# Chunk 0's keys fetched behind its other inputs, and its state sums of all batches made late in one tile

## The chip, the cores and the metric

The kernel runs on one core of one Trainium2 chip. The metric is device time in microseconds (us) of the slowest core, here the only one. A run lists its time, the span of the core in its trace (about 1.7 us less than the time) and the mean clock that TensorE was granted (1.000 is full). Runs count as fast within 1.5% of the fastest of the same kernel.

## The reference, cut to what matters

A retention layer (a linear recurrence with one decay per head), then an MLP with a leaky ReLU:

```python
# q, k, v: (4 batches, 8 heads, 768 tokens, 64)
for t in range(S):
    state = gamma * state + k[:, :, t] (outer) v[:, :, t]     # one 64x64 state per batch and head
    y[:, :, t] = scale * q[:, :, t] @ state
x = y as (3072 tokens, 512)
h = x @ w_in                       # 512 -> 2048
out = np.maximum(0.01 * h, h) @ w_out
```

## The kernel before: the parts that matter

The tokens are cut into six chunks of 128. Within a chunk the recurrence becomes matrix products: *scores* (k with q, both with dimensions first), a causal *mask* on VectorE, *values* (masked scores with decayed v), and for the chunks after it the *state sums* (k with v, both with tokens first). TensorE writes all of them into PSUM, its result memory; VectorE *takes* the values of a batch from there, times the decay, as the MLP's input x. The MLP uses a seven-product scheme, but the first products are *direct* so that they can begin with half of the inputs. Weights arrive as 64-bit floats in pieces of 512 KB and are rounded on ScalarE (three "powers" steps) and VectorE (three "mantissa" steps).

```python
def load(c, b, place=None, between=lambda: None):
    ...
    nc.sync.dma_start(out=x, in_=qk[c, b])       # 512 KB: q and k, dimensions first
    between()
    nc.sync.dma_start(out=y, in_=kv[c, b])       # 512 KB: k and v, tokens first

def state(c, b):
    y = heads.pop((c, b))[1]
    sp = for_state(sums_at[c, b])                # the free half of the bank that holds the values
    for a in range(HP) if c < NC - 1 else ():
        for j in range(2):
            nc.tensor.matmul(sp[ts(j, 64), a, :], lhsT=y[:, 0, 2 * a + j, :],
                             rhs=y[:, 1, 2 * a + j, :], start=False, stop=True, ...)

def keep_busy(n):                                # "warming": bf16 matmuls on zeros, nobody reads the result
    for _ in range(n):
        nc.tensor.matmul(idle..., lhsT=nothing[:, 0:128], rhs=nothing, ...)

# the start, in program order
load(0, 0) ; load(0, 1) ; load_piece(0) ; load_piece(1) ; load(0, 2) ; ...   # decay rates in between
keep_busy(8); score(0, 0); masked(0, 0); decay_v(0, 0, nc.vector); keep_busy(6)
values(0, 0); score(0, 1); decay_v(0, 1, nc.vector); masked(0, 1); next_powers()
state(0, 0); taken(0, 0, x); keep_busy(2)
values(0, 1); state(0, 1); taken(0, 1, x); next_powers(); next_mantissas(); next_powers()
...
keep_busy(2); decay_v(0, 2); score(0, 2); keep_busy(1); masked(0, 2)   # this decay on GpSimd
steps = direct(0, 0, x, ...); next(steps)                              # the first direct product
values(0, 2); state(0, 2); next_mantissas(); decay_v(0, 3); next(steps); ...
```

Of the kernel before, what the change touches and what calls it, by code (L numbers as in the profile page):

```python
# [23 lines left out]
def kernel(  # L24
# [35 lines left out]
    nc = tc.nc  # L60
# [13 lines left out]
    mask = const.tile([128, 128], FP32, name="mask")  # L74
    dec = const.tile([128, HP * C + H + HP], FP32, name="dec")

    st = [const.tile([128, HP, D], FP32, name=f"st{b}") for b in range(B)]



# [6 lines left out]
    def unit_tile(k, name):  # L87
        if k in LATE:
            return work.tile([128, 7, 2, 256], FP32, tag=f"late{k}", name=name)
        return const.tile([128, 7, 2, 256], FP32, name=name)  # L90
# [23 lines left out]
    heads = {}  # L114
    AHEAD = 2

    def load(c, b, place=None, between=lambda: None):

        if place is None:
            x = work.tile([128, 2, HP, C], FP32, tag="qk", bufs=AHEAD, name=f"qk_{c}_{b}")  # L120
            y = work.tile([128, 2, H, D], FP32, tag="kv", bufs=AHEAD, name=f"kv_{c}_{b}")
        else:
            flat = place.rearrange("p i k n -> p (i k n)")
            half = 2 * HP * C
            x = flat[:, 0:half].rearrange("p (s a t) -> p s a t", s=2, a=HP)
            y = flat[:, half : 2 * half].rearrange("p (s h d) -> p s h d", s=2, h=H)
        heads[c, b] = x, y
        nc.sync.dma_start(out=x, in_=qk[c, b])
        between()
        nc.sync.dma_start(out=y, in_=kv[c, b])  # L130

    def decay_v(c, b, engine=nc.gpsimd):
        v = heads[c, b][1][:, 1]
        if engine is not nc.scalar:
            engine.tensor_tensor(out=v, in0=v, in1=gk.unsqueeze(2).to_broadcast([128, H, D]),
                                 op=ALU.mult)
        else:
            for h in range(H):
                engine.activation(v[:, h], v[:, h], AF.Identity, scale=gk[:, h : h + 1])
# [6 lines left out]
    def score(c, b):  # L146

        x = heads[c, b][0]
        ps = scores[c, b] = two_banks(f"ap_{c}_{b}")
        for a in range(HP):  # L150
            for j in range(2):
                nc.tensor.matmul(ps[:, j, a, :], lhsT=x[ts(j, 64), 1, a, :],  # L152
                                 rhs=x[ts(j, 64), 0, a, :])

    def masked(c, b):
        am = work.tile([128, 2, HP, C], FP32, tag="am", bufs=2, name=f"am_{c}_{b}")
        nc.vector.tensor_tensor(  # L157
            out=am.rearrange("p j a t -> p (j a) t"),
            in0=scores[c, b].rearrange("p j a t -> p (j a) t"),
            in1=mask.unsqueeze(1).to_broadcast([128, H, C]), op=ALU.mult)  # L160
        scores[c, b] = am
# [5 lines left out]
    def reads(c, b):  # L167
        x = heads[c, b][0]
        ps = sums_at[c, b] = two_banks(f"yp_{c}_{b}")
        for j, m, i, a in pairs if c > 0 else ():  # L170
            nc.tensor.matmul(ps[ts(i, 64), j, m, :], lhsT=st[b][ts(j, 64), a, :],  # L171
                             rhs=x[ts(j, 64), 0, a, :], start=(m == 0), stop=False,
                             skip_group_check=True)

    def values(c, b):
        y, am, ps = heads[c, b][1], scores.pop((c, b)), sums_at[c, b]
        for j, m, i, a in pairs:
            nc.tensor.matmul(ps[ts(i, 64), j, m, :], lhsT=y[:, 1, 2 * a + j, :],  # L178
                             rhs=am[:, j, a, :], start=(c == 0 and m == 0), stop=True,
                             skip_group_check=True)  # L180

    def for_state(ps):
        return ps[:, 0, HP // 2 :, :].rearrange("p a (two d) -> p (a two) d", two=2)

    def state(c, b):
        y = heads.pop((c, b))[1]
        sp = for_state(sums_at[c, b])
        for a in range(HP) if c < NC - 1 else ():
            for j in range(2):
                nc.tensor.matmul(sp[ts(j, 64), a, :], lhsT=y[:, 0, 2 * a + j, :],  # L190
                                 rhs=y[:, 1, 2 * a + j, :], start=False, stop=True,
                                 skip_group_check=True)

    def taken(c, b, xb):

        ps = sums_at.pop((c, b))
        th, o = divmod(b * C, N)
        blocks = xb.rearrange("p (kh th) k n -> p kh th k n", th=2)[:, :, th, :, ds(o, C)]
        nc.vector.tensor_tensor(out=blocks, in0=ps[:, :, 0 : HP // 2, :], in1=gq, op=ALU.mult)  # L199
        sp = for_state(ps)  # L200
        if c < NC - 1:
            if c > 0:
                nc.vector.tensor_tensor(out=st[b], in0=st[b], in1=sp, op=ALU.add)
            nc.vector.tensor_tensor(out=st[b], in0=st[b] if c > 0 else sp,
                                    in1=gc.unsqueeze(2).to_broadcast([128, HP, D]), op=ALU.mult)

    def products(c, bs):
# [29 lines left out]
    def load_piece(n, place=None):  # L237
        if n >= N_PIECES:
            return
        if not f64:  # L240
            nc.sync.dma_start(out=piece(n), in_=weights[n].rearrange("p (h n) -> p h n", h=2))
            return
        if place is None:
            tag, bufs = ("raw", 3) if n < N_PIECES - 4 else (("qk", "kv")[n % 2], AHEAD)
            raws[n] = work.tile([128, W], I64, tag=tag, bufs=bufs, name=f"raw{n}")
        else:
            raws[n] = place.bitcast(I64)
        nc.sync.dma_start(out=raws[n], in_=weights[n])

    def next_powers():  # L250
        n = done["powers"]
        done["powers"] += 1
        if n < N_PIECES and f64:
            powers(n)
# [106 lines left out]
    def direct(c, u, x, g, th):  # L361


        banks = [psum.tile([128, 2, N], FP32, tag="ff", bufs=4, name=f"d{r}_{c}_{th}")
                 for r in range(2)]
        for step in range(4):
            kh, k = divmod(step, 2)
            for r in range(2):
                for i in range(2):
                    nc.tensor.matmul(  # L370
                        banks[r][:, i, :], lhsT=block(2 * u, r + 2 * kh)[:, k, ts(i, 128)],
                        rhs=x[:, 2 * kh + th, k, :], start=(step == 0 and i == 0),
                        stop=(step == 3), skip_group_check=True)
                if step == 3:
                    nc.scalar.activation(g[:, 2 * r + th], banks[r], AF.Prelu, alpha=0.01)
            yield
# [93 lines left out]
    def new_o(c):  # L470
        return work.tile([128, 4, 2, N], FP32, tag="o", bufs=2, name=f"o_{c}")
# [36 lines left out]
        return {i: [round_piece] for i in steps}  # L508

    rates = HP * C  # L510
    load(0, 0, between=lambda: nc.sync.dma_start(out=dec[:, rates:], in_=decay[:, rates:]))
    load(0, 1, between=lambda: nc.sync.dma_start(out=dec[:, :rates], in_=decay[:, :rates]))
    load_piece(0)
    load_piece(1)
    load(0, 2, new_o("in2"))
    load_piece(2)
    load_piece(3, tile_x("words").rearrange("p i k n -> p (i k n)")[:, 0 : 2 * W])
    load(0, 3, new_o("in3"))
    load(1, 0, unit_tile(LATE[2], "in10"))
    load(1, 1, unit_tile(LATE[1], "in11"))  # L520
    load(1, 2, unit_tile(LATE[0], "in12"))
    nc.vector.memset(mask, 1.0)
    nc.gpsimd.affine_select(out=mask, in_=mask, compare_op=ALU.is_ge, fill=0.0,
                            base=0, pattern=[[1, 128]], channel_multiplier=-1)
# [14 lines left out]
    def keep_busy(n):  # L539
        for _ in range(n):  # L540
            nc.tensor.matmul(idle.rearrange("p i n -> p (i n)"), lhsT=nothing[:, 0:128],
                             rhs=nothing, start=True, stop=True, skip_group_check=True)
# [2 lines left out]
    score(0, 0)  # L545
    masked(0, 0)
    decay_v(0, 0, nc.vector)
    keep_busy(6)
    reads(0, 0)
    values(0, 0)  # L550
    score(0, 1)
    decay_v(0, 1, nc.vector)
    masked(0, 1)
    next_powers()
    state(0, 0)
    taken(0, 0, x)
    keep_busy(2)
    reads(0, 1)
    values(0, 1)
    state(0, 1)  # L560
    taken(0, 1, x)
    next_powers()
    next_mantissas()
    next_powers()
    load(1, 3)
    keep_busy(2)
    decay_v(0, 2)
    score(0, 2)
    keep_busy(1)
    masked(0, 2)  # L570
    steps = direct(0, 0, x, parts[0][1], 0)
    next(steps)
    reads(0, 2)
    values(0, 2)
    state(0, 2)
    next_mantissas()
    decay_v(0, 3)
    next(steps)
    taken(0, 2, x)
    next_mantissas()  # L580
    score(0, 3)
    masked(0, 3)
    next_powers()
    next(steps)
    next_mantissas()
    reads(0, 3)
    values(0, 3)
    state(0, 3)
    decay_v(1, 0, nc.scalar)
    run(steps, {})  # L590
    taken(0, 3, x)
# [3 lines left out]
    def scored_later(b):  # L595
        score(1, b)
        masked(1, b)

    steps = direct(0, 0, x, parts[0][1], 1)
    next(steps)  # L600
    scored_later(0)
    decay_v(1, 1, nc.scalar)
    next(steps)
# [160 lines left out]
```

## Time and profile before

| | |
|---|---|
| timed runs | 673.15, 673.17, 673.52 us |
| the profiled run | 675.22 us, span 673.5, mean clock 0.997 |
| TensorE busy | 664.6 us, 99% of the span |
| first direct product starts | 18.11 us |

The prediction shows the views that carry it. One more is needed here: the timeline just ahead of the first direct product d, in the profiled run of the kernel before. A line gives start, length, engine, line of the kernel, operation, output and inputs with their shapes, and in brackets the idle time before it and what ended that.

```profile
16.09 0.39 PE L541 MATMUL idle<-t 128*128 128x512 bf16 x1
...
16.21 1.30 POOL L135 TENSOR_TENSOR o_in<-o_in,dec 128x512 f32<-128x512 f32 x1 [14.78 <-DMA o_in<-in_kv_dram]
16.71 1.34 DVE L303 SCALAR_TENSOR_TENSOR w<-w,z 128x512 f32<-128x512 f32 x1
```

TensorE's last warming matmul ends at 16.48 and d starts at 18.11, so TensorE is empty for 1.6 us. In that time GpSimd's decay of batch 2's values and VectorE's last mantissa step lie beside each other and both are long.

### The profile page before, as it was taken

The page shows a single profiled execution, that of the slowest core. Times are in us where ns is not written, and L with a number is a line of the kernel's source. Part 1 is how long each engine was busy: PE and PEld are TensorE (multiplying, and loading weights), DVE is VectorE, ACT ScalarE, POOL GpSimd, SP SyncE. Part 2 cuts the span into 40 slices and gives each one's busy share as a digit, 9 for nine tenths or more (in the row PEclk, how much of TensorE's full clock was granted, in tenths as well). Part 3 has the DMA queues.
Part 4 walks back from the last instruction along what each step waited for, and adds up shares of the span by engine and source line. Part 5 has one row for each costly group of instructions (what it writes and reads, how often), then busy time and mean ns, then how long its engine had stood idle before and what let it go on. Part 6 is the DMA issues. An engine that isn't in the chain of part 4 may idle for free.

```text
span 673.5 us, 9628 instructions
## 1 busy us (share of the span) xinstructions
PE 664.6 (99%) x4131; PEld 576.9 (86%) x4131; DVE 370.9 (55%) x566; ACT 170.4 (25%) x303; POOL 21.3 (3%) x23
## 2 busy tenths in 40 slices
PE   7999999999999999999999999999999999999997
PEld 4788888888888888888888888888888888888886
DVE  4878768889889775513733623553531444341342
ACT  2454456436352002211301211210221120221210
POOL 0100000000000110000100100100100000000000
PEclk9899999999999999999999999999999999999999
DMA  8922231231411544002102200301300000000001
GB/s 333 393 72 64 64 124 63 90 99 62 157 64 62 189 171 143 1 1 75 52 16 72 102 1 1 126 0 63 126 1 0 2 0 29 35 1 1 0 1 62
DMA packets 15306, 49.12 MB, mean 73 GB/s; under 512 B 1824, under 2 KB 1824, under 8 KB 15264
## 3 DMA queue, kind: packets, MB, share of 16 engines
q1 hardware_dynamic: 15264, 48.51, 20.2%
q8 instruction: 32, 0.52, 0.3%
q14 instruction: 10, 0.08, 0.0%
HBM read 42.21 MB, written 6.29 MB: 72 GB/s over the span
## 4 chain that ended last, share of the span: by engine, by line
PE 97%; DMA 1%; DVE 1%; SPq 0%; issue 0%; DVEq 0%
PE B_o L351 12%; PE A_o L351 12%; PE C_o L351 12%; PE C_h L351 11%; PE B_h L351 11%; PE A_h L351 11%; PE D_o L351 6%; PE D_h L351 6%; PE d L370 5%; PE yp L178 3%; PE ap L152 3%; PE yp L171 2%; PE yp L190 1%; DMA kv<-in_kv_dram 1%; DVE w L303 0%
## 5 line engine op out<-in xcount | busy, mean ns | idle before, releaser
L351 PE MATMUL A_h<-x,w 128*128 128x256 f32 x352 | 83.2, 379 | 0.0
L351 PEld LDWEIGHTS A_h<-x,w 128*128 128x128 f32 x352 | 66.9, 190 | 9.1
L351 PE MATMUL A_o<-g,w 128*128 128x256 f32 x288 | 68.0, 379 | 0.0
L383 ACT ACTIVATE g<-g 128x512 f32<-128x512 f32 x66 | 40.2, 631 | 87.7 <-DVE g L307 87.7
L351 PEld LDWEIGHTS A_o<-g,w 128*128 128x128 f32 x288 | 54.7, 190 | 7.4
L388 ACT COPY m<-A_h 128x512 f32<-128x512 f32 x22 | 12.8, 583 | 139.9 <-PE A_h L351 100.5
L307 DVE TENSOR_TENSOR m<-m,B_o 128x512 f32<-128x512 f32 x16 | 11.0, 685 | 65.9 <-PE B_o L351 65.9
L307 DVE TENSOR_TENSOR m<-m,B_h 128x512 f32<-128x512 f32 x22 | 15.1, 686 | 57.0 <-PE B_h L351 57.0
L199 DVE TENSOR_TENSOR x<-yp,dec 128x512 f32<-128x512 f32 x24 | 16.5, 689 | 50.5 <-PE yp L190 38.2
L351 PE MATMUL C_h<-t,w 128*128 128x256 f32 x176 | 42.2, 383 | 0.0
L351 PE MATMUL B_h<-x,w 128*128 128x256 f32 x176 | 42.2, 383 | 0.0
L351 PE MATMUL D_h<-t,w 128*128 128x256 f32 x176 | 41.6, 379 | 0.0
L351 PE MATMUL C_h<-x,w 128*128 128x256 f32 x176 | 41.6, 379 | 0.0
L351 PE MATMUL B_h<-t,w 128*128 128x256 f32 x176 | 41.6, 379 | 0.0
L351 PEld LDWEIGHTS D_h<-t,w 128*128 128x128 f32 x176 | 33.4, 190 | 4.5
L351 PEld LDWEIGHTS C_h<-x,w 128*128 128x128 f32 x176 | 33.4, 190 | 4.5
L351 PEld LDWEIGHTS B_h<-t,w 128*128 128x128 f32 x176 | 33.4, 190 | 4.5
L351 PEld LDWEIGHTS C_h<-t,w 128*128 128x128 f32 x176 | 32.9, 190 | 5.0
L310 DVE TENSOR_TENSOR gd<-g,gd 128x512 f32<-128x512 f32 x48 | 36.2, 753 | 1.8
L351 PEld LDWEIGHTS B_h<-x,w 128*128 128x128 f32 x176 | 32.9, 190 | 4.9 <-issue 0.3
L157 DVE TENSOR_TENSOR am<-ap,mask 128x1024 f32<-128x1024 f32 x24 | 28.6, 1220 | 12.0 <-PE ap L152 11.8
L351 PE MATMUL B_o<-gd,w 128*128 128x256 f32 x144 | 34.0, 379 | 0.0
(108 smaller groups left out, 1046.6 us busy)
## 6 DMA issues: line engine op xcount, KB each, us to landing
raw<-in_weights_dram SPq DMA_DIRECT2D x31, 512.0 KB, 3.8
qk<-in_qk_dram SPq DMA_DIRECT2D x19, 512.0 KB, 4.2
kv<-in_kv_dram SPq DMA_DIRECT2D x19, 512.0 KB, 5.2
out_dram<-o SPq DMA_DIRECT2D x24, 256.0 KB, 2.1
in<-in_qk_dram SPq DMA_DIRECT2D x3, 512.0 KB, 10.6
in<-in_kv_dram SPq DMA_DIRECT2D x3, 512.0 KB, 10.6
o_in<-in_qk_dram SPq DMA_DIRECT2D x2, 512.0 KB, 9.9
o_in<-in_kv_dram SPq DMA_DIRECT2D x2, 512.0 KB, 10.2
```

Source lines behind the costliest of these rows:

```text
L152: nc.tensor.matmul(ps[:, j, a, :], lhsT=x[ts(j, 64), 1, a, :], rhs=x[ts(j, 64), 0, a, :])
L157: nc.vector.tensor_tensor(out=am.rearrange("p j a t -> p (j a) t"), in0=scores[c, b].rearrange("p j a t -> p (j a) t"), in1=mask.unsqueeze ...
L171: nc.tensor.matmul(ps[ts(i, 64), j, m, :], lhsT=st[b][ts(j, 64), a, :], rhs=x[ts(j, 64), 0, a, :], start=(m == 0), stop=False, skip_group_ ...
L178: nc.tensor.matmul(ps[ts(i, 64), j, m, :], lhsT=y[:, 1, 2 * a + j, :], rhs=am[:, j, a, :], start=(c == 0 and m == 0), stop=True, skip_grou ...
L190: nc.tensor.matmul(sp[ts(j, 64), a, :], lhsT=y[:, 0, 2 * a + j, :], rhs=y[:, 1, 2 * a + j, :], start=False, stop=True, skip_group_check=True)
L199: nc.vector.tensor_tensor(out=blocks, in0=ps[:, :, 0 : HP // 2, :], in1=gq, op=ALU.mult)
L307: nc.vector.tensor_tensor(out=out, in0=a, in1=b, op=ALU.add)
L310: nc.vector.tensor_tensor(out=out, in0=a, in1=b, op=ALU.subtract)
L351: nc.tensor.matmul(ps[:, i, :], lhsT=block(w, sa)[:, k, ts(i, 128)], rhs=rhs[:, k, :], start=(first and i == 0 and n == 0 and k == 0), sto ...
L370: nc.tensor.matmul(banks[r][:, i, :], lhsT=block(2 * u, r + 2 * kh)[:, k, ts(i, 128)], rhs=x[:, 2 * kh + th, k, :], start=(step == 0 and i ...
L383: nc.scalar.activation(g[:, i], g[:, i], AF.Prelu, alpha=0.01)
L388: nc.scalar.copy(out=got["m1"], in_=ps)
```

## The change

Its intent: only v, not k, is needed with tokens first to get chunk 0's values out. So k (256 KB per batch) is fetched behind everything else that chunk 0 needs, and the state sums are made when all four k are there. Chunk 0 has no older state, so the four sums can be multiplied by the decay in one VectorE operation, if the four states lie in one tile. Warming matmuls, the order of the small operations and the place of two loads of chunk 1 were changed along with it. In the cut below, lines of one kind are joined with semicolons.

```diff
-    st = [const.tile([128, HP, D], FP32, name=f"st{b}") for b in range(B)]
+    states = const.tile([128, B, HP, D], FP32, name="states")
+    st = [states[:, b] for b in range(B)]
...
+    def load_v(c, b):
+        nc.sync.dma_start(out=heads[c, b][1][:, 1], in_=kv[c, b][:, 1])
+    def load_k(c, b):
+        nc.sync.dma_start(out=heads[c, b][1][:, 0], in_=kv[c, b][:, 0])
...
+    def first_states_taken(ps):
+        flat = ...
+        nc.vector.tensor_tensor(out=states, in0=flat..., in1=gc (broadcast), op=ALU.mult)
...
-    load(0, 0, ...)  load(0, 1, ...)  load_piece(0)  load_piece(1)  load(0, 2, ...)
-    load_piece(2)  load_piece(3, ...)  load(0, 3, ...)  load(1, 0, ...) ...
+    load_qk(0, 0)  (small decay row)  load_v(0, 0)  load_qk(0, 1)  (decay rates)  load_v(0, 1)
+    load_piece(0)  load_qk(0, 2)  load_v(0, 2)  load_piece(1)  load_piece(2)  load_piece(3, ...)
+    load_qk(0, 3)  load_v(0, 3)  load_k(0, 0..3)  load(1, 0, ...) ...
...
-    keep_busy(6); reads(0, 0); values(0, 0); score(0, 1); decay_v(0, 1); masked(0, 1)
-    next_powers(); state(0, 0); taken(0, 0, x); keep_busy(2); values(0, 1); state(0, 1) ...
+    keep_busy(4); score(0, 1); values(0, 0); masked(0, 1); decay_v(0, 1); keep_busy(3)
+    next_powers(); taken(0, 0, x); values(0, 1); taken(0, 1, x) ...
...
-    keep_busy(2) ... keep_busy(1)
+    score(0, 2); masked(0, 2); keep_busy(4)          # right ahead of the first direct product
...
-    decay_v(0, 3)
+    decay_v(0, 3, nc.scalar)
...
+    values(0, 3); first_state(0, sums0); first_state(1, sums0)      # behind three direct steps
...
+    first_state(2, sums0); first_state(3, sums0); first_states_taken(sums0)
```

More of the change, by code (lines that the diff above doesn't have):

```diff
@@ L115, with place_for @@
     AHEAD = 2
-    def load(c, b, place=None, between=lambda: None):
+    def place_for(c, b, place=None):
         if place is None:
@@ L127, in load, with load_qk @@
         heads[c, b] = x, y
-        nc.sync.dma_start(out=x, in_=qk[c, b])
-        between()
-        nc.sync.dma_start(out=y, in_=kv[c, b])
+    def load_qk(c, b):
+        nc.sync.dma_start(out=heads[c, b][0], in_=qk[c, b])
+    def load_v(c, b):
+        nc.sync.dma_start(out=heads[c, b][1][:, 1], in_=kv[c, b][:, 1])
+    def load_k(c, b):
+        nc.sync.dma_start(out=heads[c, b][1][:, 0], in_=kv[c, b][:, 0])
+    def load(c, b, place=None):
+        place_for(c, b, place)
+        load_qk(c, b)
+        nc.sync.dma_start(out=heads[c, b][1], in_=kv[c, b])
     def decay_v(c, b, engine=nc.gpsimd):
@@ L169, in reads @@
         ps = sums_at[c, b] = two_banks(f"yp_{c}_{b}")
-        for j, m, i, a in pairs if c > 0 else ():
+        for j, m, i, a in pairs:
             nc.tensor.matmul(ps[ts(i, 64), j, m, :], lhsT=st[b][ts(j, 64), a, :],
@@ L175, in values @@
     def values(c, b):
+        if c == 0:
+            sums_at[c, b] = two_banks(f"yp_{c}_{b}")
         y, am, ps = heads[c, b][1], scores.pop((c, b)), sums_at[c, b]
@@ L188, in state, with sums_of, first_state @@
         for a in range(HP) if c < NC - 1 else ():
-            for j in range(2):
-                nc.tensor.matmul(sp[ts(j, 64), a, :], lhsT=y[:, 0, 2 * a + j, :],
-                                 rhs=y[:, 1, 2 * a + j, :], start=False, stop=True,
-                                 skip_group_check=True)
+            sums_of(sp, y, a)
+    def sums_of(sp, y, a, start=False):
+        for j in range(2):
+            nc.tensor.matmul(sp[ts(j, 64), a, :], lhsT=y[:, 0, 2 * a + j, :],
+                             rhs=y[:, 1, 2 * a + j, :], start=start, stop=True,
+                             skip_group_check=True)
+    def first_state(b, ps):
+        y = heads.pop((0, b))[1]
+        sp = ps[:, b // 2].rearrange("p a t -> p (a t)")[:, ds(b % 2 * HP * D, HP * D)]
+        for a in range(HP):
+            sums_of(sp.rearrange("p (a d) -> p a d", d=D), y, a, start=(b % 2 == 0 and a == 0))
+    def first_states_taken(ps):
+        flat = ps.rearrange("p j a t -> p (j a t)").rearrange("p (ba d) -> p ba d", d=D)
+        nc.vector.tensor_tensor(
+            out=states,
+            in0=flat.rearrange("p (b a) d -> p b a d", b=B),
+            in1=gc.unsqueeze(1).unsqueeze(3).to_broadcast([128, B, HP, D]), op=ALU.mult)
     def taken(c, b, xb):
@@ L199, in taken @@
         nc.vector.tensor_tensor(out=blocks, in0=ps[:, :, 0 : HP // 2, :], in1=gq, op=ALU.mult)
-        sp = for_state(ps)
-        if c < NC - 1:
-            if c > 0:
-                nc.vector.tensor_tensor(out=st[b], in0=st[b], in1=sp, op=ALU.add)
-            nc.vector.tensor_tensor(out=st[b], in0=st[b] if c > 0 else sp,
+        if 0 < c < NC - 1:
+            nc.vector.tensor_tensor(out=st[b], in0=st[b], in1=for_state(ps), op=ALU.add)
+            nc.vector.tensor_tensor(out=st[b], in0=st[b],
                                     in1=gc.unsqueeze(2).to_broadcast([128, HP, D]), op=ALU.mult)
@@ L510 @@
     rates = HP * C
-    load(0, 0, between=lambda: nc.sync.dma_start(out=dec[:, rates:], in_=decay[:, rates:]))
-    load(0, 1, between=lambda: nc.sync.dma_start(out=dec[:, :rates], in_=decay[:, :rates]))
+    place_for(0, 0)
+    place_for(0, 1)
+    place_for(0, 2, new_o("in2"))
+    place_for(0, 3, new_o("in3"))
+    load_qk(0, 0)
+    nc.sync.dma_start(out=dec[:, rates:], in_=decay[:, rates:])
+    load_v(0, 0)
+    load_qk(0, 1)
+    nc.sync.dma_start(out=dec[:, :rates], in_=decay[:, :rates])
+    load_v(0, 1)
     load_piece(0)
+    load_qk(0, 2)
+    load_v(0, 2)
     load_piece(1)
-    load(0, 2, new_o("in2"))
     load_piece(2)
     load_piece(3, tile_x("words").rearrange("p i k n -> p (i k n)")[:, 0 : 2 * W])
-    load(0, 3, new_o("in3"))
+    load_qk(0, 3)
+    load_v(0, 3)
+    for b in range(B):
+        load_k(0, b)
     load(1, 0, unit_tile(LATE[2], "in10"))
     load(1, 1, unit_tile(LATE[1], "in11"))
-    load(1, 2, unit_tile(LATE[0], "in12"))
     nc.vector.memset(mask, 1.0)
@@ L547 @@
     decay_v(0, 0, nc.vector)
-    keep_busy(6)
-    reads(0, 0)
+    keep_busy(4)
+    score(0, 1)
     values(0, 0)
-    score(0, 1)
+    masked(0, 1)
     decay_v(0, 1, nc.vector)
-    masked(0, 1)
+    keep_busy(3)
     next_powers()
-    state(0, 0)
     taken(0, 0, x)
-    keep_busy(2)
-    reads(0, 1)
     values(0, 1)
-    state(0, 1)
     taken(0, 1, x)
@@ L564 @@
     next_powers()
-    load(1, 3)
-    keep_busy(2)
     decay_v(0, 2)
     score(0, 2)
-    keep_busy(1)
     masked(0, 2)
+    keep_busy(4)
     steps = direct(0, 0, x, parts[0][1], 0)
     next(steps)
-    reads(0, 2)
     values(0, 2)
-    state(0, 2)
     next_mantissas()
-    decay_v(0, 3)
+    load(1, 2, unit_tile(LATE[0], "in12"))
+    next_powers()
+    decay_v(0, 3, nc.scalar)
     next(steps)
     taken(0, 2, x)
+    score(0, 3)
     next_mantissas()
-    score(0, 3)
     masked(0, 3)
-    next_powers()
     next(steps)
     next_mantissas()
-    reads(0, 3)
+    load(1, 3)
     values(0, 3)
-    state(0, 3)
+    sums0 = two_banks("sums0")
+    first_state(0, sums0)
+    first_state(1, sums0)
     decay_v(1, 0, nc.scalar)
@@ L600 @@
     next(steps)
+    first_state(2, sums0)
+    first_state(3, sums0)
+    first_states_taken(sums0)
     scored_later(0)
```

## The prediction

> **What bounds the kernel now.** I read the page first, then the chain of waits in order of time, then busy time and granted clock in two-microsecond stretches, then the early transfers in order of time.
>
> The page: busy shares and the clock row (40 slices of 16.8 us, tenths of full clock).
>
> ```profile
> PE 664.6 (99%) x4131; PEld 576.9 (86%) x4131; DVE 370.9 (55%) x566; ACT 170.4 (25%) x303; POOL 21.3 (3%) x23
> ...
> PEclk9899999999999999999999999999999999999999
> DMA  8922231231411544002102200301300000000001
> ```
>
> TensorE is busy 99% of 673.5 us; only the first two slices have an unfilled clock or full DMA. So whatever can be won lies in the first 34 us. The chain that ended last says where (start, length, what):
>
> ```profile
> 3.12 7.89 DMA kv<-in_kv_dram
> ...
> 11.64 1.23 DVE am L157
> ...
> 12.92 1.09 PE yp L178 x16
> 14.01 0.49 PE yp L190 x16
> ...
> 15.13 0.41 DVE st L204
> 15.55 0.34 DVE w L299
> ...
> 15.92 0.71 DVE w L301
> ...
> 16.71 1.36 DVE w L303
> ...
> 18.11 3.51 PE d L370 x8
> 21.62 1.14 PE yp L178 x16
> 22.77 0.46 PE yp L190 x16
> 23.23 1.92 PE d L370 x8
> ```
>
> Until 18.11 the chain hops between a transfer, VectorE and TensorE; from 18.11 on, where the first direct product (d) starts, every later piece I looked at is TensorE. The end is therefore "time at which d starts" plus "TensorE work that is left". Two things stand out. The start waits for token-major k and v of batch 1 (the kv transfer landing at 11.0). And the first d group takes 3.51 for eight matmuls where the next takes 1.92. Busy time of PE, PEld, DVE, ACT, POOL, then clock, DMA share, GB/s:
>
> ```profile
> 14.00:16.00 2.00, 2.00 (x36) 1.45 (x30) 1.44 (x4) 1.94 (x4) 0.00 (x0) 1.00 1.03 414
> 16.00:18.00 2.00, 0.47 (x5) 0.10 (x1) 1.90 (x3) 0.77 (x2) 1.30 (x1) 1.00 1.01 397
> 18.00:20.00 2.00, 1.89 (x5) 1.59 (x6) 1.97 (x4) 1.93 (x4) 0.00 (x0) 0.61 1.04 416
> 20.00:22.00 2.00, 2.00 (x10) 1.17 (x11) 0.94 (x2) 1.26 (x2) 0.34 (x1) 0.54 1.01 401
> 22.00:24.00 2.00, 2.00 (x35) 1.85 (x31) 0.72 (x2) 0.00 (x0) 0.70 (x1) 1.00 1.05 418
> ```
>
> TensorE is nearly idle from 16 to 18, and then its clock is half for about 3.4 us. The first d product runs in that hole. DMA is saturated at some 410 GB/s, so bytes in the queue ahead of an input are time.
>
> **What the Trainium skill says.**
> 1. "TensorE: Matmul & The Clock Gate", Part 1: activity windows of about 3.4 us, free-running, each deciding between half and full clock. The trace agrees in size: the stretches above give a half-clock interval of 3.4 us, with both edges inside one two-microsecond stretch each. That its phase is free is not seen here: the three timed runs lie within 0.4 us. The page speaks of an idle window; here a window with about half its time busy was enough.
> 2. "DMA: Bandwidth & Descriptors", Specifications: transfers of at least 512 B per descriptor run at line rate. The split transfers have 2 KB rows; the 256 KB load of the decay rates has the same row size, and the stretch from 8 to 10 us, in which by the working below its last rows landed, moved 412 GB/s, the usual rate.
> 3. "SBUF — State Buffer", Who interferes with whom: VectorE with two SBUF inputs and a GpSimd operation that reads SBUF exclude each other, the later one waits. The trace agrees: the last mantissa step (L303) took 1.34 us beside a 1.30 us GpSimd decay, 0.69 alone.
> 4. "PSUM — Partial Sum Buffer", The four PSUM rules: only the first matmul in a bank clears it; sums for two batches share one bank, and the new code sets the flag only on the first. This is correctness, not time.
>
> **The change part by part.**
>
> *Loads.* Steady issues stand 1.28 us apart (9.75, 11.03, 12.31, 13.59 for 512 KB each), so 256 KB is 0.64 us. Before, the queue is qk0, small decay row, kv0, qk1, rates, kv1, weight piece 0, piece 1, qk2, kv2, pieces 2 and 3, qk3, kv3. After, each kv of chunk 0 is only its v half, qk2 and v2 stand ahead of piece 1, and the four k halves come behind v3. From kv1's landing at 11.02 backwards, qk1 landed near 9.1 (11.02 - 1.28 - 0.64). New landings: qk1 9.1 - 0.64 = 8.46; v1 8.46 + 0.64 + 0.64 = 9.74; piece 0 11.02; qk2 12.3; v2 12.9; piece 1 14.2; piece 2 15.5; piece 3 16.8; qk3 18.1; v3 18.7; the four k by 21.3. Total bytes are unchanged, so chunk 1's inputs land as before (first kv about 24.2).
>
> *The road to d.* Program order is now scores 0, four warming matmuls, scores 1, values 0, three warming, values 1, with masked 1 ahead of decay 1 on VectorE and no state sums.
> - Scores 0 start at 4.88 as before (behind the eight cold warming matmuls), mask 0 ends at 7.39; decay 0 follows without its 0.47 wait, to 8.1.
> - Scores 1: qk1 at 8.46 + 1.16 = 9.6. Mask 1 starts 0.13 after, 9.75 + 1.23 = 11.0; decay 1 starts 0.09 before that end and takes 0.69: 11.6. Values 1: 11.65 + 1.05 = 12.7.
> - The taking of batch 1: 12.75. Before, from this operation (14.53) to d (18.11) were 3.58 us. Of these 0.33 was the state product (L204), which leaves. 0.65 was the L303 collision (1.34 - 0.69). Without either, d starts at 12.75 + 2.6 = 15.35.
> - Collision again: GpSimd's decay of v2 starts at 12.9 and needs 1.04, to about 13.95. The first mantissa step (L299) would start at 13.35 with SBUF input in a two-port form, then L301 with two. They would wait up to 0.6, so d at 15.95. I take the middle, 15.6: a gain of 18.11 - 15.6 = 2.5 us.
> - Piece 0 lands at 11.02 and its three ScalarE steps need 1.95 (12.97), before they are wanted.
>
> *The clock.* Now four warming matmuls (0.98 at full clock) stand behind scores 2, right up to d: values 1, scores 2 and warming cover 11.65 to about 14.8. So the hole of 16 to 18 shrinks to under a microsecond, and the half clock should not strike d. That saves 3.51 - 1.92 = 1.6 us.
>
> *Moved work.* Two batches' state sums, 0.46 each, stood ahead of d, inside waits; now all four stand behind it. Cost on a full TensorE: 0.93 us. The other two were already behind d. The multiply that takes all four (128 x 1024 from PSUM, like the mask's 1.23) replaces four of 0.415: VectorE saves about 0.4 us, off the path.
>
> *Does TensorE stay full after d?* With d at T: values 2 at T+1.9, piece 1 needed at T+2.95. VectorE does mask 2 (1.14 per start) and three mantissa steps (0.46 + 0.79 + 0.69): T+3.05, so about 0.1 of a wait. Piece 2 is needed at T+5.96 and ready near T+5.5; piece 3 at T+9.84, ready near T+9.2. ScalarE's last power step ends at about 20, then decay of v3 (2.0): 22, needed at T+7.9 = 23.5. The k halves (by 21.3) are needed from T+8.9 = 24.5. None becomes a bound.
>
> *Sum:* 673.17 - 2.5 - 1.6 + 0.93 + 0.3 (small waits) = **670.3 us**, 0.4% less.
>
> **Rivals.**
> - *Half clock moves instead of leaving.* After scores 0 and four warming matmuls TensorE now idles from 7.0 to 8.46; before, six kept it until 7.4 and the idle time ended at 8.6. The window there would be about 64% busy; windows of 70% and over stayed at full clock and one of 52% did not. If it falls there, scores 1 and values take about 1.1 us longer each way to d: 671.4. If instead a window around d is still judged idle, the 1.6 is not won: 671.9.
> - *The transfer was hidden anyway:* mask 1 and decay 1 come one after the other, so early v1 (9.74) waits for mask 1 (11.0). For it: the order on VectorE. Then only qk1's 0.64 counts, not the 1.28 of v1; the road above already has this, which is why I do not credit more.
> - *Early transfers run better than the queue rate.* From 2 to 8 us only 281 to 340 GB/s moved; smaller rows could let qk1 land at 7.5. Then d starts near 14.8: 669.5.
> - *VectorE becomes the bound* after d, since pieces 1 to 3 are rounded between masks and takings while TensorE starts sooner. Margins are 0.5 us or so; if they fail once or twice, plus 0.5 to 1: 671.
>
> **Range and chances.** All rivals move the time by one or two microseconds around 670.3, and they partly exclude each other: 668.8 to 672.3 holds it 8 times in 10. Two per cent is 13.5 us, and the whole stretch before d is only 18 us, half of it fixed by the first transfers; faster by over 2% gets 0.01, slower by over 2% 0.01, within 2% 0.98.
>
> **What would show it.** d's first start near 15.6 (14.8 to 16.0) in the chain; its first eight matmuls near 1.9 and clock 1.00 in every stretch from 14 to 24; the state sums as four groups of 0.46 between d groups, with no idle time before them; L299 or L301 longer than 0.42 or 0.69 beside GpSimd's first decay; TensorE full from d to the end. Wrong if d starts after 17, if a half-clock stretch remains anywhere after 5, or if new idle time shows after d, above all before the first d of piece 1 or the first states' reading in chunk 1.

## The result, and the profile after

| | before | after |
|---|---|---|
| median of the first rounds, us | 673.31 (673.15 to 673.52, 4 runs) | 672.10 (671.93 to 672.46, 4 runs) |
| profiled run, us | 675.22 | 671.97 |
| span of the profiled run, us | 673.5 | 670.3 |
| first direct product in the profile, us | 18.11 | 15.17 |

The ratio is 0.9982, with a 95% interval of 0.9965 to 1.0000. Ratios are the mean time of one kernel's fast runs over that of the other's of the same rounds, so not quite the ratio of the medians quoted. The gain is 1.2 us; 2.9 were forecast.

The two profiled runs, however, differ by 3.2 us, close to the forecast. That contradiction is the clue. First the profile after. The page of the changed kernel, the busy row and the clock row:

```profile
PE 663.0 (99%) x4131; PEld 575.8 (86%) x4131; DVE 369.2 (55%) x563; ACT 172.1 (26%) x311; POOL 20.3 (3%) x22
...
PEclk9999999999999999999999999999999999999999
```

The unfilled clock digit in the second slice is gone. The chain that ended last, in the changed kernel (start, length, what):

```profile
3.60 6.63 DMA raw<-in_weights_dram
...
12.31 1.29 DVE w L329
...
13.63 0.70 DVE w L331
...
14.43 0.70 DVE w L333
...
15.17 1.99 PE d L400 x8
17.17 1.02 PE yp L192 x16
18.19 1.97 PE d L400 x8
...
24.20 0.93 PE sums L207 x32
25.13 3.65 PE d L400 x16
28.78 1.08 PE sums L207 x32
```

The first direct product starts 2.94 us earlier, and its eight matmuls take 1.99 instead of 3.51. The four state sums stand behind it and cost 2.01 together. The chain comes to d through piece 0 (landing at 10.2) and its rounding on ScalarE, which the prediction had as done before it is wanted; the taking of batch 1 on VectorE ends within 0.2 us of it, and in the two later profiles of this kernel the chain comes through the scores instead. The same stretches as before (busy time of PE, PEld, DVE, ACT, POOL; clock; DMA share; GB/s):

```profile
14.00:16.00 2.00, 0.83 (x4) 0.75 (x5) 1.90 (x3) 1.94 (x4) 0.00 (x0) 1.00 1.01 405
16.00:18.00 2.00, 2.00 (x22) 1.54 (x20) 1.86 (x4) 1.91 (x5) 0.00 (x0) 1.00 1.04 389
18.00:20.00 2.00, 2.00 (x12) 1.44 (x8) 1.83 (x4) 1.97 (x6) 0.00 (x0) 1.00 1.07 396
20.00:22.00 2.00, 2.00 (x21) 1.71 (x21) 1.40 (x2) 1.19 (x5) 0.00 (x0) 1.00 1.03 401
```

TensorE is full from d on and its clock never falls. And the timeline ahead of d in the changed kernel:

```profile
12.27 1.04 POOL L147 TENSOR_TENSOR o_in<-o_in,dec 128x512 f32<-128x512 f32 x1 [10.84 <-DMA raw<-in_weights_dram]
12.31 1.28 DVE L329 TENSOR_SCALAR w<-raw 128x512 uint32<-128x512 uint32 x1
...
12.76 1.04 PE L582 MATMUL idle<-t 128*128 128x512 bf16 x4
...
15.17 1.99 PE L400 MATMUL d<-x,w 128*128 128x256 f32 x8 [1.38 <-DVE w L333]
```

GpSimd's decay, which needs v2, now meets the first mantissa step instead of the last: 1.28 us instead of 0.42.

So in the two profiled runs the forecast steps show up: d earlier by some 3 us, its clock full, the sums behind it. In the timed runs the gain does not. The theory: the half-clock interval of the profile before (about 1.7 us of time: 3.4 us at half speed) struck that one execution and not the timed ones. The rival: every run before has it, and the gain was lost elsewhere.

### The profile page after: what moved, and what is told of

It reads as the page before. It is cut to its first block, busy times and chain, and to the rows that moved or that the text cites. A ratio compares the mean times of both kernels' runs of the same rounds, so it can differ in the third digit from the quotient of the medians.

```text
span 670.3 us, 9636 instructions
## 1 busy us (share of the span) xinstructions
PE 663.0 (99%) x4131; PEld 575.8 (86%) x4131; DVE 369.2 (55%) x563; ACT 172.1 (26%) x311; POOL 20.3 (3%) x22
## 4 chain that ended last, share of the span: by engine, by line
PE 97%; DMA 1%; DVE 1%; SPq 0%; ACT 0%; issue 0%; DVEq 0%
PE B_o L381 12%; PE A_o L381 12%; PE C_o L381 12%; PE C_h L381 12%; PE B_h L381 12%; PE A_h L381 11%; PE D_o L381 6%; PE D_h L381 6%; PE d L400 4%; PE ap L164 3%; PE yp L192 3%; PE yp L183 2%; PE yp L207 1%; DMA raw<-in_weights_dram 1%; PE sums L207 0%; DVE w L329 0%
## 5 line engine op out<-in xcount | busy, mean ns | idle before, releaser
L231 DVE TENSOR_TENSOR x<-yp,dec 128x512 f32<-128x512 f32 x24 | 16.5, 688 | 48.7 <-PE yp L207 35.6
```

The source lines that it names most:

```text
L231: nc.vector.tensor_tensor(out=blocks, in0=ps[:, :, 0 : HP // 2, :], in1=gq, op=ALU.mult)
```

## The experiments

Twelve kernels ran, in three calls. In each call the kernels share one chip and the runs of the kernel before.

### Is the half clock in every run? The kernel before, unchanged

> The kernel before, unchanged, to see time, span and granted clock of every run. Theory A (the half-clock interval of the profiled run before is not typical: that run took 675.22 us, the other four 673.15 to 673.52, about 3.41 us x 0.5 = 1.7 us less): most runs show a clock of 1.000 and 673.2 to 673.5 us with a span near 671.6; a run with a clock of about 0.997 takes about 1.7 us more. Theory B (every run has the half-clock interval, and the 1.9 us extra of that run is something else, such as recording): all runs show about 0.997 and 673.3 us in time, and the gain of the change is smaller for another reason.

Its five runs gave 673.43 us (673.16 to 673.58), the nine runs of the kernel before beside it 673.37 (673.13 to 673.57); ratio 1.0001. Each run lists time, span and clock:

```
e1:      673.16 671.5 1.000 | 673.47 671.7 1.000 | 673.16 671.4 1.000 | 673.43 671.7 1.000 | 673.58 671.9 1.000
before:  clocks 0.999 or 1.000 in all nine, spans 671.4 to 671.8
```

The spans are 671.4 to 671.9, not the 673.5 of the first profile. Two stretches of the new profile of the same kernel:

```profile
16.00:18.00 2.00, 0.29 (x1) 0.29 (x2) 1.90 (x3) 0.90 (x2) 1.11 (x1) 1.00 1.04 406
18.00:20.00 2.00, 2.00 (x14) 1.51 (x15) 1.86 (x4) 1.94 (x4) 0.00 (x0) 1.00 1.01 408
```

The gap on TensorE is there as before, but the clock stays at 1.00. (It is again about 1.6 us: one warming matmul has no record in this trace, but its weight load stands at 15.68.) Its chain of waits has the first direct product at full speed:

```profile
17.71 1.99 PE d L370 x8
```

Theory A holds. The kernel before ran 41 times, these five and the profiled one included. Three runs had the half clock: 675.22, 674.79 and 675.19 us, each with a clock of 0.997. Only the first of them was profiled; where it fell in the other two is not recorded. On average it costs 3/41 of 1.7, some 0.1 us, not 1.6. A clock of 0.999 instead of 1.000 is something else: in all six kept traces that have it, the clock falls behind TensorE's last matmul (in the changed kernel's second profile at 669.2 us, the last matmul ends at 666.5), where it costs TensorE nothing.

### The gap filled, and nothing else

```diff
-    keep_busy(1)
+    keep_busy(8)
     masked(0, 2)
```

> The kernel before with eight warming matmuls instead of one behind the scores of batch 2, so that TensorE is not idle from 16.5 to 18.1 us; nothing else moves (they end before the rounded piece 0 is ready). Theory A: timed runs equal to before (ratio 0.9995 to 1.0005), clock 1.000 in all runs, span about 671.7 also where it is profiled. Theory B: 1.6 us faster than before (ratio 0.9976).

673.39 us (673.12 to 673.73), ratio 1.0000. The stretches of its profile:

```profile
16.00:18.00 2.00, 1.80 (x10) 0.70 (x8) 1.90 (x3) 0.76 (x2) 1.30 (x1) 1.00 1.02 401
18.00:20.00 2.00, 1.92 (x8) 1.44 (x8) 1.97 (x4) 1.91 (x4) 0.00 (x0) 1.00 1.03 412
```

TensorE now has work for 1.80 of the 2 us ahead of d, and the time does not move. Theory A predicted 0.9995 to 1.0005, the rival 0.9976. Taking the gap away buys nothing in an ordinary run, so the change could not win 1.6 us by it either.

### Can the gap cause it at all? The gap widened, in both kernels

The changed kernel without its last four warming matmuls:

```diff
     masked(0, 2)
-    keep_busy(4)
```

> The changed kernel without the four warming matmuls ahead of the first direct product, so that TensorE has no work from about 12.8 to 15.2 us. If an idle stretch ahead of that product lets the clock fall whenever it fills enough of one 3.4 us activity window, some or most of the runs now show a clock near 0.997 and 673.8 us (1.7 more), and the profile, if it catches one, has the first direct products at half clock. If TensorE needs a whole idle window, all runs stay at 1.000 and 672.1.

Six runs, with time, span and clock:

```
671.63 669.9 1.000 | 672.13 670.4 1.000 | 672.18 670.4 0.999 | 673.42 671.7 0.997 | 674.57 672.8 0.997 | 674.23 672.5 0.997
```

Three of the six have a clock of 0.997, and they are 1.2 to 2.9 us longer than the others. The kernel before without the warming around the scores of batch 2:

```diff
     load(1, 3)
-    keep_busy(2)
...
-    keep_busy(1)
     masked(0, 2)
```

> The kernel before without the three warming matmuls around the scores of batch 2, so that the gap ahead of the first direct product is 2 us and the 0.6 us ahead of the scores are empty too. If the half clock strikes when one activity window is filled too little, a third or more of the runs now show a clock near 0.997 and about 675 us, the rest stays at 673.3. If the 675.22 us run of before had another cause, all stay at 673.3.

```
672.75 671.0 1.000 | 673.40 671.7 1.000 | 673.68 672.0 0.999 | 674.76 673.0 0.997 | 674.83 673.1 0.997 | 674.82 673.1 0.997
```

In its profile the gap ahead of d is 1.97 us, with another 0.51 us ahead of the scores. Again three of six have it, about 1.5 us longer (means of 674.80 and 673.28; about 675 and 673.3 were expected). In the changed kernel with its warming matmuls none of 14 runs had it, and none of the 30 runs of its five variants told of below, which all leave TensorE work there. So the warming matmuls do keep the clock up, and what they change is how often it falls. Both profiles caught runs at full clock; that the half clock of the others fell at d is inferred from the edit, which touches nothing else.

What decides for a single run stays open. The profiled run without the last warming kept the full clock:

```profile
14.84 2.00 PE L400 MATMUL d<-x,w 128*128 128x256 f32 x8 [2.14 <-DVE w L333]
```

TensorE was idle for 2.14 us here and d ran at full speed, while in the first profile of before an idle stretch of 1.6 us was enough. So the length of the gap alone does not decide. How it falls between two of the free-running activity windows that "TensorE: Matmul & The Clock Gate", Part 1, describes could, and would differ from run to run. The packed traces let this be tried: the times at which their recorded clock changes inside a run are whole multiples of 3.413 us apart (in the first profile of before full clock from 4.77 for 13.65 us, half for 3.41, full for 651.95), so windows can be laid out from them. In the struck run the window ahead of the fall (15.01 to 18.42) has TensorE busy for 52%. In the second profile of the same kernel one (15.99 to 19.41) is busy for 52% too, with the missing matmul counted, and in the profile without the last warming one (11.05 to 14.46) for 48%; both kept the full clock. If the edges are shifted earlier by up to a whole window, there is at every shift some window as empty as the struck one that kept it. So the busy share of one window, by which the prediction told safe windows from unsafe ones, does not decide either.

### The split of k and v undone, the rest of the change kept

```diff
     def load_v(c, b):
-        nc.sync.dma_start(out=heads[c, b][1][:, 1], in_=kv[c, b][:, 1])
+        nc.sync.dma_start(out=heads[c, b][1], in_=kv[c, b])
...
-    for b in range(B):
-        load_k(0, b)
```

> The changed kernel with k and v of chunk 0 fetched together again, each at the place of its v (the other order of loads and the late state sums stay). The inputs ahead of the first direct product then come 1.28 us later (two k halves, 0.64 us each) at batch 1's values and piece 0. If the split is what brought the start forward, it starts at 15.9 to 16.5 instead of 15.17 and the time is 0.7 to 1.3 us longer, 672.8 to 673.4, so the gain of the change is gone. If the engines' chain (masks one after the other) sets the start, it moves by less than 0.4 us.

673.35 us (673.10 to 673.53), ratio to before 1.0000. From its chain of waits:

```profile
2.17 6.74 DMA qk<-in_qk_dram
...
15.07 1.35 DVE w L333
...
16.47 1.99 PE d L400 x8
```

The first direct product starts at 16.47, inside the expected 15.9 to 16.5 and 0.8 to 1.3 us later than in three profiles of the changed kernel (15.17, 15.42, 15.71). All of the net gain hangs on the split. The other part of the earlier start, 1.2 us against the 17.71 of the kernel before, is left for the new order and for the state sums taken out of the way; no run tells these two apart. It pays only for those sums where they now stand: from d to the end of the span it is 655.1 us here and 653.7 in the second profile of the kernel before.

### GpSimd's collision with the rounding of piece 0

The decay of batch 2's values goes to ScalarE:

```diff
-    decay_v(0, 2)
+    decay_v(0, 2, nc.scalar)
     score(0, 2)
```

> The changed kernel with the decay of batch 2's values on ScalarE instead of GpSimd. If GpSimd's operation (1.04 us) is what stretched the first mantissa operation from 0.42 to 1.28 us ahead of the first direct product, that operation returns to 0.42, the product starts at about 14.3 instead of 15.17 and the kernel gains 0.8 us: about 671.3. If the stretch has another cause, or ScalarE's two extra microseconds delay the powers of piece 1, nothing is gained (672.1) or 0.5 us lost.

673.52 us (672.57 to 673.89), so no gain over the changed kernel, whose first four runs had 672.1. They were run at other times. The timeline says why:

```profile
12.83 0.42 DVE L329 TENSOR_SCALAR w<-raw 128x512 uint32<-128x512 uint32 x1
...
14.82 1.99 PE L400 MATMUL d<-x,w 128*128 128x256 f32 x8 [0.58 <-DVE w L333]
...
17.92 2.10 PE L192 MATMUL yp<-am,o_in 128*64 128x128 f32 x16 [1.10 <-ACT o_in L151]
```

The mantissa step is back at 0.42, so it was the collision. (d starts at 14.82 and not at 14.3, because the scores of batch 1 came 0.5 us later than in the first profile of the changed kernel.) But at this place in the program ScalarE does the decay behind the powers of pieces 1 and 2, and the values of batch 2 wait for it. The same move, placed ahead of the powers of piece 1:

```diff
     taken(0, 1, x)
+    decay_v(0, 2, nc.scalar)
     next_powers()
...
-    decay_v(0, 2)
     score(0, 2)
```

> The changed kernel with the decay of batch 2's values on ScalarE, this time ahead of the powers of piece 1 (the earlier try had it behind the powers of piece 2, where the values of batch 2 waited for it). GpSimd's collision with the first mantissa operation goes, the first direct product starts near 14.4 to 14.8 instead of 15.2 and nothing waits behind it: 0.4 to 0.8 us under the changed kernel, 671.3 to 671.7. If ScalarE's chain then holds piece 1 up, the gain is lost at the second direct product.

671.96 us (670.85 to 672.58), ratio to before 0.9972 (0.9960 to 0.9984). The changed kernel gave:

> The changed kernel unchanged, in five rounds. Theory (every term of the prediction held but the clock's, because the half-clock interval struck only one run of the kernel before): time 671.9 to 672.4, that is 1.1 to 1.5 us under before, ratio 0.9978 to 0.9984, span about 670.4, clock 1.000 in all runs. Rival (the gain is larger and the first four runs were unlucky): 671.5 or less.

672.80 us (672.25 to 673.43), ratio 0.9988 (0.9976 to 0.9999): slower than the 672.4 at the upper end of what was expected, and with more scatter than in the first four runs. Both kernels once more:

> The changed kernel once more, beside its variants on one chip. It has given 672.1 (four runs) and 672.8 (five). Theory (the whole gain is the earlier first direct product minus 1.1 us of moved state sums, and the start scatters with the landing of the first transfers): 672.0 to 672.9, ratio 0.9980 to 0.9992.

> The changed kernel with batch 2's decay on ScalarE ahead of the powers of piece 1, again. If its 0.8 us lead over the changed kernel of the last call was the collision (0.6 us in the profiles) and not scatter, it is again 0.5 to 0.9 us under it, ratio to before 0.9968 to 0.9980.

The changed kernel gave 672.58 us (672.14 to 672.60), ratio 0.9982 (0.9970 to 0.9994). With the decay on ScalarE it was 671.40 us (671.02 to 672.33), ratio 0.9968 (0.9956 to 0.9980). The lead over the changed kernel is 0.8 and 1.2 us, against 0.6 to 0.9 us of collision in the profiles (1.00, 1.07 and 1.28 us instead of 0.42). So this version beats both kernels, by about 0.3% against the one before. From the timeline of the last one:

```profile
12.53 2.02 ACT L151 ACTIVATE o_in<-o_in,dec 128x64 f32<-128x64 f32 x8
12.88 0.42 DVE L329 TENSOR_SCALAR w<-raw 128x512 uint32<-128x512 uint32 x1
...
14.87 1.99 PE L400 MATMUL d<-x,w 128*128 128x256 f32 x8 [0.58 <-DVE w L333]
```

Here d starts at 14.87, in the first profile of this version at 15.53, later than the 14.4 to 14.8 that were expected and than in two profiles of the changed kernel. What differs there is when the first inputs land: from the start of batch 1's scores to d it is 6.91 us in both profiles of this version, against 7.77, 7.50 and 7.55 in those of the changed kernel. So the road is shorter by the collision, 0.6 to 0.9 us, wherever it begins.

### The state sums put back ahead of the first direct product

There TensorE had warming matmuls only, so real work would fit. Two tries, both on top of the last versions, with the sums of batches 0 and 1 in a PSUM bank of their own. The first has the decay on ScalarE and fetches the two k behind v2:

```diff
     load_v(0, 2)
+    load_k(0, 0)
+    load_k(0, 1)
     load_piece(1)
...
-    keep_busy(4)
+    keep_busy(1)
+    first_state(0, sums01...)
+    first_state(1, sums01...)
```

> As the one with the decay on ScalarE, and the state sums of batches 0 and 1 made ahead of the first direct product in place of three of the four warming matmuls, in a bank of their own, their keys fetched behind the values of batch 2. The 0.93 us of state sums that the change put on the full TensorE then lie in a gap: 0.9 us under the kernel with the decay placed, 670.4 to 670.8. If the keys land too late (after 13.5 us) or pieces 1 to 3, which now come 1.28 us later, hold a direct product up, half of it or more is lost.

672.12 us (672.11 to 672.45), ratio 0.9978: no better than without. Its chain:

```profile
8.31 7.20 DMA raw<-in_weights_dram
...
18.17 0.70 DVE w L339
...
18.92 1.13 PE d L406 x4
```

Piece 1 landed at 15.5 us, its rounding was late and the second direct product waited 0.65 us for it; a further 0.23 us was lost at the fourth. The second try fetches piece 1 ahead of v2 and leaves the decay of batch 2 on GpSimd, where it should meet the mask rather than a mantissa step:

```diff
     load_piece(0); load_qk(0, 2)
+    load_k(0, 0); load_k(0, 1)
+    load_piece(1)
     load_v(0, 2)
-    load_piece(1)
```

> State sums of batches 0 and 1 ahead of the first direct product as in the earlier try, but with piece 1 fetched behind their keys and ahead of batch 2's values, whose decay stays on GpSimd. Piece 1 then lands 0.64 us later than in the changed kernel instead of 1.28, and GpSimd runs beside the mask, which reads PSUM, instead of the first mantissa operation. If both hold, the first direct product starts near 14.4 to 14.8, the second no longer waits, and 0.9 us of sums are gone: 1.2 to 1.7 us under the changed kernel of the same call, about 671.0. If GpSimd meets another mantissa operation or piece 1 is still late, 0.5 us or less.

672.32 us (671.90 to 673.01), ratio 0.9981, 0.3 us under the changed kernel where 1.2 to 1.7 had been expected. From its timeline:

```profile
15.06 1.04 POOL L147 TENSOR_TENSOR o_in<-o_in,dec 128x512 f32<-128x512 f32 x1 [13.62 <-DMA o_in<-in_kv_dram]
...
15.66 0.72 DVE L335 TENSOR_SCALAR w<-raw 128x512 uint32<-128x512 uint32 x1
...
17.97 1.99 PE L406 MATMUL d<-x,w 128*128 128x256 f32 x8 [0.28 <-DVE w L339]
```

The first direct product did start at 14.67. But GpSimd stretched a mantissa step again, now the first one of piece 1 (0.72 instead of 0.42), and piece 1 landed 0.8 us later than in the first profile of the changed kernel (its powers start at 14.27 instead of 13.49). So the second direct product waited 0.28 us and the fourth 0.24. The end of this profiled run has a loss of another kind: from TensorE's last matmul to the end of the span it is 4.9 us instead of 4.0, with one store of the output landing after 3.2 us instead of 2.1; whether other runs had it is not known. In both tries a later transfer, and in the second a longer VectorE operation too, reached the path at the second direct product; room for the sums has to be paid for.

## Why the prediction came out as it did

**What bounds the kernel.** Right. The time is the start of d plus the TensorE work that is left: from d to the first output product TensorE took 45.77 us in the second profile of the kernel before (17.71 to 63.48) and 46.86 in the changed one (15.17 to 62.03). The difference, 1.09, is the size of the moved state sums (2.01 for four now, 0.92 for the two that stood behind d before), and TensorE waits for nothing in either stretch. From there to TensorE's last matmul both take 604.2 us.

**The loads and the road to d.** Right in the sum. Forecast: d at 15.6, 2.5 us earlier. Measured: 15.17, 15.42 and 15.71 in three profiles of the changed kernel, against 18.11, 17.71 and 18.08 in profiles of the kernel before (the last with its gap filled, which does not touch this road). The means are 15.43 and 17.97, so 2.5 us (with the two kernels with the wider gap, 14.84 and 17.28, it is 2.5 as well). That the sum fits so well is partly luck: two terms inside were off and cancelled. Scores of batch 1 began at 7.40, 7.92 and 8.16 instead of 8.46, because the first transfers came better than worked back from the later ones (a rival named this). And the collision with GpSimd cost 0.86, 0.58 and 0.65 us, at or above the full 0.6 instead of the half that was booked. From these scores to d the road took 7.5 to 7.8 us instead of 7.1.

**The clock.** This is the step that failed: "the half clock should not strike d. That saves 3.51 - 1.92 = 1.6 us." The mechanism is real: the changed kernel never showed the half clock in 14 runs, and with the gap widened 6 of 12 runs do. But the saving was booked against a profiled run that was itself the exception, 3 of 41. In an ordinary run before, d already takes 1.99 us, and filling its gap gives a ratio of 1.0000. The term is worth about 0.1 us as a mean over runs and nothing in a median. The evidence was at hand: the profiled run before took 675.22 us, the timed ones 673.15 to 673.52, and its span of 673.5 was as long as their whole time although a span is 1.7 us shorter. The prediction subtracted from 673.17, a time without the half clock, what only the 675.22 us run could have given back.

**Moved work.** Right in mechanism, a little small: 1.09 us instead of 0.93.

**Waits behind d.** 0.3 us were booked. TensorE is full behind d in the changed kernel's three profiles, so there are none. A term that was not booked: from TensorE's last matmul to the end of the span it is 4.0 us in these three profiles and 3.75 in all four of the kernel before and its variants. Why these 0.25 us are there is not known.

**The sum again.** 673.17 - 2.5 + 1.09 + 0.25 = 672.0. Measured were 672.1 in the first rounds, and gains of 1.2, 0.5 and 1.3 us by the medians of the three sets of rounds, where 1.2 is due. The 0.5 of the second set is 0.7 short; d's start scatters by about as much (15.17 to 15.71 in the three profiles, 14.84 without the last warming), but no profile caught such a run, so its cause stays open.

**The rivals.** The half clock did not move to an earlier window (14 runs at 0.999 or 1.000). The transfer was not hidden: with k and v together d is 0.8 to 1.3 us later. VectorE did not become the bound behind d in the changed kernel; in the two tries with early sums, where less time was left, it did, together with the later piece 1.

**What stays open.** Besides what tips the clock in a given run: some runs of the kernel before took 673.9 to 674.4 us at a clock of 0.999 or 1.000, and the changed kernel scattered from 671.9 to 673.4. Part of this may be a late warm-up at the start, which the mean clock does not count: in the packed traces the record of the clock begins only when it becomes full, 4.22 to 7.32 us after the start of the span in the fourteen profiles, and the later this is, the longer the scores of batch 0 take (1.16 to 2.08 us). In the profile of the changed kernel in the second call the stretch from 5 to 6 us is listed as

```profile
5.00:6.00 1.00, 1.00 (x10) 1.00 (x12) 0.00 (x0) 0.00 (x0) 0.00 (x0) 1.00 0.49 168
```

with a clock of 1.00, but the scores that run in it took 2.01 us instead of the 1.09 of later ones:

```profile
4.99 2.01 PE ap L164 x16
```

In this profile the delay is on the road to d, because the chain goes from these scores over warming matmuls straight to those of batch 1; in most profiles of this order, batch 1's scores wait longer for their transfer. Whether it explains the slower timed runs was not tested.

## What to carry to other kernels

Before a saving is booked against something that a profile shows once, compare the profiled run's own time and span with the timed runs: if it is longer than they are, what it shows extra is not in the baseline. Fetching by need, even by splitting one transfer in two, is worth its bytes at the queue's rate where a start waits on a full queue, but work that is pushed out of a wait onto a full engine costs its whole length. An engine that is nearly idle can still sit on the path by stretching what runs beside it: one 1 us GpSimd operation cost up to 0.9 us of start, and moving it to ScalarE, at the right place in the program, won 0.8 and 1.2 us.

## What the Trainium skill lacked or had wrong

- "TensorE: Matmul & The Clock Gate", Part 1, has in its table of states an idle window of about 3.4 us before the clock halves. Here an idle stretch of 1.6 us was enough in one profiled run, and 2.14 us was not in another; the kernel with the stretch of 1.6 us tipped in 3 of 41 runs, the two with 1.97 and 2.14 us in 3 of 6 each. The page also tells of short idle times that make the clock swing, without sizes or odds; what decides it lacks. The half-clock interval of about 3.4 us agrees.
- No page says that the mean clock of a profile may count the time before the first recorded change as full. In one profile matmuls of a 1.09 us group took 2.01 us under a listed clock of 1.00; the record of the clock began at 7.01 us there.
- No page gives how unevenly a kernel's first transfers come. With the same order of loads, the scores that wait for the second input began between 7.3 and 8.6 us, and two-microsecond stretches from 2 to 6 us moved 159 to 344 GB/s in the fourteen profiles, against some 410 later.
- "SBUF — State Buffer", Who interferes with whom, was right for both forms met here; it has no size for them. A 0.42 us one-input step took 1.00 to 1.28 us and a 0.69 us two-input step 1.34 us beside one GpSimd operation.
